# One assignment's one-hot products in two parts: the bank of the squares' sums and spare columns of a score tile

## The chip, the cores and the metric

The kernel runs on one core of one Trainium2 chip. The metric is the device time of one execution in microseconds (us); several executions are timed and their median is given. A core has five engines with an instruction stream each: PE (matrix products), DVE, ACT and POOL (elementwise work), and SP, which here only issues transfers. They wait for one another through semaphores.

## What is computed

Four batches of eight heads of attention, 768 positions with 64 values each, in which a query sees only keys of its own cluster; then a feed-forward network with the Mish function on the 3072 x 512 result.

```python
q_assign = np.argmax(np.einsum('bhsd,hcd->bhsc', q_n, c_n), axis=-1)
k_assign = np.argmax(np.einsum('bhsd,hcd->bhsc', k_n, c_n), axis=-1)
mask = q_assign[:, :, :, None] == k_assign[:, :, None, :]
scores = np.where(mask, scale * np.matmul(q, k.transpose(0, 1, 3, 2)), -1000000000.0)
attn = np.exp(scores - np.max(scores, axis=-1, keepdims=True))
attn = attn / (np.sum(attn, axis=-1, keepdims=True) + 1e-09)
x = np.matmul(attn, v)              # then to (3072, 512)
h = x @ w_in                        # (512, 2048)
sp = np.where(h > 20.0, h, np.log1p(np.exp(np.minimum(h, 20.0))))
g = h * np.tanh(sp)
out = g @ w_out                     # (2048, 512)
```

## The kernel before

**Units and score tiles.** The attention is cut into 96 units (a head and a third of its queries) of two halves of 128 queries. For unit i, half a, PE makes the scores in a PSUM tile s{i}_{a} of two banks: `scores_own` (L670) the products of q and k, `scores` (L690) on top of them the products of Z and T, whose last 16 rows are one-hot cluster rows, which stand for the mask. Of the 512 columns of each bank, scores fill 384; the other 128 are spare. DVE takes the row maximum m (`rowmax`, L701), ACT the exponential p (`expo`, L715). In the early units (0 to 23) PE transposes p into tiles q of the tag "H" (`p_lo`, L763), ACT and DVE copy these to SBUF (`ptrans`, L784 and L782), and `pv` (L806) multiplies with v for two units at a time into a tile o of the tag "M"; pv 10 covers units 20 and 21. Later units are transposed by DMA (L786). A half such as unit 22, half 0 is called s22_0, m22_0, exp22_0 and q22_0 below, by tile.

**Assignments.** For four heads at a time, PE multiplies q and k with the centroids (`assign_mm`, L572), DVE turns the result, takes the maximum over clusters and compares (`assign_turn`, `assign_max`, `assign_hot`, `assign_back`, L583 to L604), PE forms the one-hot rows of the four heads out of it (`assign_put`, L628), DVE evicts them into a tile stg (`assign_stg`, L649), and SP copies 16 rows at a time into Z and T of each head (`hot_copy`, L660 and L661). Assignment 2 serves heads 8 to 11, whose first scores are those of unit 24.

**PSUM.** Eight banks: tag "S" two tiles of two banks each (the scores, and put of the assignments after the first), "M" one bank, "H" two banks (the transposes q, later the products h of the first matrix, L901 to L903), "O" one bank. Early in the program "O" holds gram, the sums of squares of the weights (L323); from unit 28 on it holds the output O of the second matrix (L1038 to L1040). A ring hands out the tiles of a tag in the order of the program: who asks for one waits until its last reader is done.

**Other work beside it.** The weights are scaled and split into two 16-bit parts by POOL (`w_low` L295, `w_hi` L360), ACT (`w_abs` L286) and DVE (`w_f32` L303, `w_lo` L366); q and k of later heads are prepared by POOL (`prep`, L500 to L521); the values' squares go through `v_sq` (ACT, L384), `v_max` (DVE, L415), `v_cross` (PE, L389), `v_peak` (DVE, L393), `v_wide` (PE, L398) into one number that scales v. v_cross writes into spare columns of s22_1, v_wide into those of s23_0.

**What sets the order.** A list ORDER of 3408 steps, written out in the kernel, gives each step its rank. `Plan` issues steps by rank and ties the instructions of each engine in that order; `pl.after` issues a step's predecessors first. So a step that waits holds up everything behind it on its engine.

Of the kernel before, what the change touches and what calls it, by code (L numbers as in the profile page):

```python
# [1672 lines left out]
p_lo 15 0, scores 16 1, w_sq 25, w_sq 26, w_sq 27, w_sq 28, p_lo 15 1, scores 17 1, scores 17 0, recip 15 1, rowmax 16  # L1673
0, rowmax 16 1, ptrans 15 0, expo 16 0, p_hi 16 0, total 16 0, recip 16 0, expo 16 1, p_hi 16 1, w_lo 6, ptrans 15 1,
rowmax 17 0, rowmax 17 1, recip 14 1, p_lo 16 0, pv 7 0, pv 7 1, pv 7 2, pv_out 14, x_lo 14, p_lo 16 1, v_sq 1 0,
w_abs 30, w_abs 29, expo 17 0, p_hi 17 0, total 17 0, recip 17 0, ptrans 16 0, w_abs 31, expo 17 1, p_hi 17 1, ptrans
16 1, total 16 1, w_low 29, prep_hi 7, prep_lo 7, w_low 31, recip 16 1, w_f32 30, w_f32 29, w_f32 31, pv_out 15, x_lo
15, w_hi 7, total 17 1, scores 18 1, p_lo 17 0, scores 18 0, w_sq 29, p_lo 17 1, w_sq 30, rowmax 18 1, ptrans 17 0,
rowmax 18 0, ptrans 17 1, w_lo 7, pv 8 0, w_sq 31, recip 17 1, w_sum 1, expo 18 0, p_hi 18 0, total 18 0, recip 18 0,
p_lo 18 0, scores 19 0, w_spread 1, w_scale 1, rowmax 19 0, expo 18 1, p_hi 18 1, ptrans 18 0, p_lo 18 1, scores 19 1,  # L1680
pv 8 1, pv 8 2, pv_out 16, x_lo 16, rowmax 19 1, ptrans 18 1, expo 19 0, p_hi 19 0, total 19 0, recip 19 0, expo 19 1,
p_hi 19 1, copy_t 7, copy_z 7, qk_load 11, qk_load 10, hot_copy 7, copy_a 7, x_move 6 1, copy_b 7, x_move 5 0,
assign_mm 2, p_lo 19 0, scores 20 0, w_hi 8, total 19 1, total 18 1, w_lo 8, pv_out 17, x_lo 17, w_hi 9, recip 19 1,
recip 18 1, assign_turn 2, prep_hi 8, ptrans 19 0, prep_lo 8, p_lo 19 1, scores 20 1, assign_max 2, rowmax 20 0,
assign_hot 2, ptrans 19 1, rowmax 20 1, assign_back 2, expo 20 0, p_hi 20 0, total 20 0, recip 20 0, expo 20 1, p_hi
20 1, pv 9 0, p_lo 20 0, scores 21 0, pv 9 1, rowmax 21 0, w_lo 9, moe_scale_h 0, pv 9 2, pv_out 18, x_lo 18, scores
# [290 lines left out]
```

## Time and profile before

| what | value |
|---|---|
| median of three timed runs | 838.34 us (838.01 to 838.62) |
| the profiled execution's own time | 836.27 us |
| its span (first to last instruction) | 834.5 us |
| PE, DVE, ACT, POOL busy | 99%, 79%, 61%, 53% |
| granted TensorE clock | 1.00 over the whole span |

The profile is of one execution. Its span is 1.77 us shorter than its own time, and that time lies 2.07 us below the median of the timed runs. A row of the order-of-time view has the start, the duration, engine, line, operation, tiles (result, arrow, inputs), shape and count, and in brackets the idle time just before it with the instruction that ended it. Instructions of one kind in a row are put together, and durations overlap where an engine pipelines, so starts are the better measure of what an instruction takes.

### The profile page before, as it was taken

How to read it: one execution, taken by the hardware profiler on the slowest of the kernel's cores; microseconds unless marked ns; L12 is line 12 of the kernel's file. 1: busy time of each engine (PE TensorE's matmuls, PEld its weight loads, DVE VectorE, ACT ScalarE, POOL GpSimd, SP SyncE). 2: the span in 40 equal slices, each digit the busy share in tenths (PEclk: the TensorE clock that was granted, in tenths of full speed). 3: DMA queues.
4: the chain of work that ended last, by engine and by line, in shares of the span. 5: the costliest groups of instructions: out<-in, count | busy, mean ns of one | idle time of the engine just before them, and what ended most of it. 6: DMA issues, size and time to landing. Idle time of an engine off the chain costs nothing.

```text
span 834.5 us, 17572 instructions
## 1 busy us (share of the span) xinstructions
PE 822.7 (99%) x6732; PEld 624.9 (75%) x6733; DVE 659.9 (79%) x1146; ACT 509.6 (61%) x872; POOL 440.6 (53%) x424
## 2 busy tenths in 40 slices
PE   7999999999999999999999999999999999999998
PEld 3787777876776777776776687686777677788887
DVE  7999999999788868688777778778887675688822
ACT  6988877766565755573765465575665564365610
POOL 4778865976675555565656356665557251110000
PEclk9999999999999999999999999999999999999999
DMA  9997843899999968878899979896979774000001
GB/s 345 284 286 228 209 124 77 162 188 169 185 183 215 175 120 177 193 152 129 149 175 187 218 147 160 156 205 133 171 132 155 131 115 90 13 1 2 1 8 70
DMA packets 257299, 125.64 MB, mean 151 GB/s; under 512 B 231136, under 2 KB 234720, under 8 KB 257216
## 3 DMA queue, kind: packets, MB, share of 16 engines
q1 hardware_dynamic: 253120, 115.54, 66.5%
q10 hardware_dynamic: 4096, 8.98, 5.2%
q8 instruction: 53, 0.87, 0.4%
q14 instruction: 30, 0.25, 0.1%
HBM read 35.72 MB, written 6.29 MB: 50 GB/s over the span
## 4 chain that ended last, share of the span: by engine, by line
PE 85%; DVE 5%; ACT 3%; DMA 3%; POOL 2%; issue 2%; ACTq 0%; DVEq 0%; POOLq 0%; SPq 0%
PE o L806 10%; PE h L901 10%; PE h L903 10%; PE h L902 10%; PE O L1038 7%; PE O L1039 7%; PE O L1040 7%; PE s L670 7%; PE s L690 6%; PE cn L991 2%; PE q L763 1%; DVE m L701 1%; PE as L572 1%; ACT p L715 1%; DMA stage<-in_w_out_dram 1%
## 5 line engine op out<-in xcount | busy, mean ns | idle before, releaser
L715 ACT ACTIVATE p<-s,m 128x768 f32<-128x768 f32 x192 | 172.8, 902 | 112.1 <-DVE m L701 46.9
L753 POOL TENSOR_SCALAR hl<-p,l 128x768 f16<-128x768 f32 x144 | 164.6, 1147 | 142.9 <-DVE l L735 73.5
L701 DVE TENSOR_REDUCE m<-s 128x1 f32<-128x768 f32 x192 | 179.7, 949 | 47.5 <-PE s L690 46.2
L770 DVE SCALAR_TENSOR_TENSOR hl<-p,l,hl 128x768 f16<-128x768 f32 x144 | 173.9, 1218 | 25.0 <-POOL hl L753 24.0
L901 PE MATMUL h<-x,w 128*128 128x256 f16 x640 | 175.0, 273 | 0.2 <-ACT pt L784 0.2
L903 PE MATMUL h<-x,w 128*128 128x256 f16 x640 | 174.4, 273 | 0.0
L902 PE MATMUL h<-x,w 128*128 128x256 f16 x640 | 174.4, 273 | 0.0
L670 PE MATMUL s<-A,B 128*128 128x384 f32 x384 | 116.4, 384 | 2.4 <-ACT p L715 1.6
L1038 PE MATMUL O<-w,g 128*128 128x512 f16 x288 | 109.9, 382 | 0.0
L1039 PE MATMUL O<-w,g 128*128 128x512 f16 x288 | 109.2, 379 | 0.0
L1040 PE MATMUL O<-w,g 128*128 128x512 f16 x288 | 109.2, 379 | 0.0
L690 PE MATMUL s<-Z,T 80*128 80x384 f32 x384 | 99.3, 340 | 0.0
L901 PEld LDWEIGHTS <-w 128*128 128x128 f16 x768 | 75.1, 98 | 20.7 <-issue 9.9
L912 ACT ACTIVATE u<-h,msch 128x512 f32<-128x512 f32 x80 | 53.7, 686 | 50.8 <-PE h L903 38.0
L902 PEld LDWEIGHTS <-w 128*128 128x128 f16 x768 | 75.3, 98 | 10.9 <-issue 0.4
L903 PEld LDWEIGHTS <-w 128*128 128x128 f16 x768 | 75.2, 98 | 8.7
L918 POOL TENSOR_SCALAR g<-u,mscg 128x512 f16<-128x512 f32 x72 | 60.5, 844 | 36.7 <-ACT u L912 29.5
L806 PE MATMUL o<-pt,v 128*64 128x256 f16 x1296 | 77.6, 274 | 0.0
L806 PEld LDWEIGHTS <-v 128*64 128x64 f16 x1296 | 67.9, 110 | 9.8 <-issue 9.3
L926 DVE SCALAR_TENSOR_TENSOR g<-u,mscg,g 128x512 f16<-128x512 f32 x72 | 67.6, 946 | 9.7 <-POOL g L918 9.7
L670 PEld LDWEIGHTS s<-A,B 128*128 128x128 f32 x384 | 64.6, 190 | 13.6 <-ACT p L715 3.5
L690 PEld LDWEIGHTS s<-Z,T 80*128 80x128 f32 x384 | 70.0, 189 | 0.1
(251 smaller groups left out, 1347.1 us busy)
## 6 DMA issues: line engine op xcount, KB each, us to landing
qk<-in_qk_dram SPq DMA_DIRECT2D x32, 384.0 KB, 4.4
stage<-in_w_in_dram SPq DMA_DIRECT2D x16, 512.0 KB, 7.3
stage<-in_w_out_dram SPq DMA_DIRECT2D x16, 512.0 KB, 5.1
vraw<-in_vP_dram SPq DMA_DIRECT2D x16, 384.0 KB, 5.4
Z<-B SPq DMA_DIRECT2D x30, 192.0 KB, 3.5
out_dram<-osb SPq DMA_DIRECT2D x18, 256.0 KB, 3.3
T<-A ACTq DMA_DIRECT2D x23, 192.0 KB, 3.9
B<-T ACTq DMA_DIRECT2D x21, 192.0 KB, 4.0
```

Source lines behind the costliest of these rows:

```text
L670: nc.tensor.matmul(s[:, j, :384], st["B", n][:, q0 : q0 + P], st["A", n][:, j * 384 : (j + 1) * 384], start=True, stop=False, skip_group_c ...
L690: nc.tensor.matmul(st["s", i, a][:, j, :384], st["T", n][: D + NCL, q0 : q0 + P], st["Z", n][: D + NCL, j * 384 : (j + 1) * 384], start=Fa ...
L701: nc.vector.tensor_reduce(m, st["s", i, a][:, :, :384], axis=AX.XY, op=ALU.max, negate=True)
L715: nc.scalar.activation(p.rearrange("p (n x) -> p n x", n=2), st["s", i, a][:, :, :384], AF.Exp, bias=st["m", i, a], scale=1.0, accum_out=l,)
L770: nc.vector.scalar_tensor_tensor(t[:, 1], p, r, t[:, 0], op0=ALU.mult, op1=ALU.subtract)
L806: nc.tensor.matmul(o[s * D : s * D + D, :256], v if early else v[:, int(part == 1)], st["pt", 2 * m + s][:, :, c + (0 if early or part < 2 ...
L901: nc.tensor.matmul(o, wh, xh, start=(c == 0), stop=False)
L902: nc.tensor.matmul(o, wh, xl, start=False, stop=False)
L903: nc.tensor.matmul(o, wl, xh, start=False, stop=(c == 3))
L1038: nc.tensor.matmul(o, gh, wh, start=(f == 0 and fi == 0), stop=False)
L1039: nc.tensor.matmul(o, gh, wl, start=False, stop=False)
L1040: nc.tensor.matmul(o, gl, wh, start=False, stop=(f == 7 and fi == 1))
```

## The change

For the third assignment (q = 2) `assign_put` asks for no tile of the tag "S". Its first 512 columns go into a tile of the tag "O", the last 256 into the spare columns of both banks of s22_0, which has to be made first. That is three products (512, 128 and 128 columns) in place of two (512 and 256), and `assign_stg` evicts it in two instructions in place of one. The other assignments stay as they were. The lines behind it move by 6 to 8 numbers (L628 is L634, L649 is L657, L670 is L678, L701 is L709, L715 is L723, L763 is L771, L784 is L792).

```diff
@@ -605,7 +605,13 @@
 
     def assign_put(q):
         pl.after(("assign_back", q), ("put_consts",))
-        if q:
+        if q == 2:
+            pl.after(("scores", 22, 0))
+            o = ps.tile([P, 512], F32, tag="O", name=f"put{q}", bufs=T["O"])
+            t = st["s", 22, 0][:, :, 384:]
+            st["put", q] = [(o, 0, 512), (t, 512, S)]
+            parts = [(o, 0, 512), (t[:, 0], 512, 640), (t[:, 1], 640, S)]
+        elif q:
             o = ps2.tile([P, 1024], F32, tag="S", name=f"put{q}")
             st["put", q] = [(o[:, :S], 0, S)]
             parts = [(o[:, :512], 0, 512), (o[:, 512:S], 512, S)]
@@ -646,7 +652,9 @@
         pl.after(("assign_put", q))
         stg = op1.tile([P, S], F32R, tag="stg", name=f"stg{q}")
         for o, c0, c1 in st["put", q]:
-            nc.vector.tensor_scalar(stg[:, c0:c1], o, 0.0, put_b, op0=ALU.max, op1=ALU.subtract)
+            t = stg[:, c0:c1]
+            t = t.rearrange("p (j x) -> p j x", j=2) if len(o.shape) == 3 else t
+            nc.vector.tensor_scalar(t, o, 0.0, put_b, op0=ALU.max, op1=ALU.subtract)
         st["stg", q] = stg
 
     def hot_copy(n):
...
```

Of the list ORDER, 340 places change (581 to 920 of 3408, from the 15th unit's end to the second pair of the feed-forward's first product); the steps are the same. The two lines with the put and the eviction, before and now:

```diff
-rowmax 21 1, w_lo 10, rowmax 22 0, ptrans 20 1, expo 21 1, p_hi 21 1, p_lo 21 0, assign_put 2, p_lo 21 1, ptrans 21 0,
-v_sq 1 3, expo 22 0, p_hi 22 0, total 22 0, recip 22 0, assign_stg 2, v_max 1, ptrans 21 1, scores 22 1, v_cross 1,
...
+21 1, rowmax 22 0, w_lo 10, ptrans 20 1, expo 21 1, p_hi 21 1, assign_put 2, p_lo 21 0, p_lo 21 1, scores 22 1, ptrans
+21 0, assign_stg 2, moe_scale_h 0, expo 22 0, ptrans 21 1, p_hi 22 0, total 22 0, recip 22 0, pv 10 0, v_cross 1, p_lo
...
```

**First place: POOL, about 100 to 109 us.** Names: stage holds raw weights (w_low, L295), qk, A and B belong to head 7 (prep). Before:

```order
L295 TENSOR_SCALAR stage_1400<-stage_1400 128x512
L500 TENSOR_SCALAR qk_478<-qk_478,scq 128x768
L503 TENSOR_SCALAR A_1650<-qk_478 128x768
L521 TENSOR_TENSOR B_1653<-qk_478,A_1650 128x768
L295 TENSOR_SCALAR stage_1405<-stage_1405 128x512
```

Now:

```order
L500 TENSOR_SCALAR qk_478<-qk_478,scq 128x768
L503 TENSOR_SCALAR A_1647<-qk_478 128x768
L521 TENSOR_TENSOR B_1650<-qk_478,A_1647 128x768
L295 TENSOR_SCALAR stage_1400<-stage_1400 128x512
L295 TENSOR_SCALAR stage_1405<-stage_1405 128x512
```

The three instructions of prep stand ahead of both weight pieces; before they stood between them, so the second piece (stage_1405) was behind all of them and the first piece too.

**Second place: PE around the put.** Names: s_1_1922 and s_0_1935 before, s_1_1920 and s_0_1925 now are s21_1 and s22_0; s_1_1996 and s_1_1983 are s22_1; q_0_0, q_0_3, q_1_0 and q_1_3 are the transposes of one half in two tiles, first of unit 20, half 1, then of unit 21. Weight loads are left out. Before:

```order
L670 MATMUL s_1_1922<-A_1650,B_1653 128x384 x2
L690 MATMUL s_1_1922<-Z_1796,T_1794 128x384 x2
L763 MATMUL q_1_0_1927<-ident,p_1_1883 128x128 x3
L763 MATMUL q_1_3_1931<-ident,p_1_1883 128x128 x3
L670 MATMUL s_0_1935<-A_1650,B_1653 128x384 x2
L690 MATMUL s_0_1935<-Z_1796,T_1794 128x384 x2
L763 MATMUL q_0_0_1963<-ident,p_0_1943 128x128 x3
L763 MATMUL q_0_3_1967<-ident,p_0_1943 128x128 x3
L628 MATMUL put_1971<-hott_1878,put_w 128x512
L628 MATMUL put_1971<-hott_1878,put_w 128x256
L763 MATMUL q_1_0_1974<-ident,p_1_1961 128x128 x3
L763 MATMUL q_1_3_1978<-ident,p_1_1961 128x128 x3
```

Now:

```order
L678 MATMUL s_0_1925<-A_1647,B_1650 128x384 x2
L698 MATMUL s_0_1925<-Z_1800,T_1798 128x384 x2
L771 MATMUL q_1_0_1930<-ident,p_1_1885 128x128 x3
L771 MATMUL q_1_3_1934<-ident,p_1_1885 128x128 x3
L634 MATMUL put_1963<-hott_1880,put_w 128x512
L634 MATMUL s_0_1925<-hott_1880,put_w 128x128
L634 MATMUL s_0_1925<-hott_1880,put_w 128x128
L771 MATMUL q_0_0_1967<-ident,p_0_1941 128x128 x3
L771 MATMUL q_0_3_1971<-ident,p_0_1941 128x128 x3
L771 MATMUL q_1_0_1975<-ident,p_1_1961 128x128 x3
L771 MATMUL q_1_3_1979<-ident,p_1_1961 128x128 x3
L678 MATMUL s_1_1983<-A_1647,B_1650 128x384 x2
```

s22_0 has moved ahead of the transposes of unit 20, the put stands ahead of those of unit 21 instead of between them, and two of its products write the tile of s22_0.

**Third place: DVE around the eviction, and ACT beside it.** Names: m_1_1954 is m21_1, m_0_1957 and m_0_1956 are m22_0, m_1_2033 and m_1_2039 are m22_1; w_951 is the split of a weight piece (w10), vsm belongs to v_max, pt to the copies of the transposes. DVE before:

```order
L701 TENSOR_REDUCE m_1_1954<-s_1_1922 128x1
L366 SCALAR_TENSOR_TENSOR w_951<-w_780,ws1r,w_951 128x1024
L701 TENSOR_REDUCE m_0_1957<-s_0_1935 128x1
L649 TENSOR_SCALAR stg_1990<-put_1971,put_b 128x768
L415 TENSOR_REDUCE vsm_1992<-vm_1284 128x1
L782 COPY pt_1982<-q_1_3_1978 128x384
L366 SCALAR_TENSOR_TENSOR w_780<-w_1085,ws1r,w_780 128x1024
L701 TENSOR_REDUCE m_1_2033<-s_1_1996 128x1
```

DVE now:

```order
L709 TENSOR_REDUCE m_1_1954<-s_1_1920 128x1
L709 TENSOR_REDUCE m_0_1956<-s_0_1925 128x1
L366 SCALAR_TENSOR_TENSOR w_951<-w_780,ws1r,w_951 128x1024
L657 TENSOR_SCALAR stg_1991<-put_1963,put_b 128x512
L657 TENSOR_SCALAR stg_1991<-s_0_1925,put_b 128x256
L463 TENSOR_SCALAR msch_1994<-vs0r,ws0r 128x1
L467 TENSOR_SCALAR mscg_1996<-vs0r,ws0r 128x1
L790 COPY pt_1988<-q_1_3_1979 128x384
L366 SCALAR_TENSOR_TENSOR w_780<-w_1085,ws1r,w_780 128x1024
L709 TENSOR_REDUCE m_1_2039<-s_1_1983 128x1
```

m22_0 has moved ahead of w10, the eviction is in two and stays behind w10, v_max has left, and the two small products msch and mscg came in. ACT before, from exp21_1 to exp22_1:

```order
L715 ACTIVATE p_1_1961,l_1944<-s_1_1922,m_1_1954 128x768
L784 COPY pt_1982<-q_0_0_1963 128x384
L784 COPY pt_1982<-q_0_3_1967 128x384
L384 ACTIVATE vq_3_1985,vm_1284<-vraw_3_1408 128x768
L715 ACTIVATE p_0_1987,l_1988<-s_0_1935,m_0_1957 128x768
L784 COPY pt_1982<-q_1_0_1974 128x384
L784 COPY pt_2059<-q_0_0_2002 128x384
L784 COPY pt_2059<-q_0_3_2006 128x384
L715 ACTIVATE p_1_2062,l_1988<-s_1_1996,m_1_2033 128x768
```

ACT now:

```order
L723 ACTIVATE p_1_1961,l_1942<-s_1_1920,m_1_1954 128x768
L792 COPY pt_1988<-q_0_0_1967 128x384
L792 COPY pt_1988<-q_0_3_1971 128x384
L723 ACTIVATE p_0_1998,l_1999<-s_0_1925,m_0_1956 128x768
L792 COPY pt_1988<-q_1_0_1975 128x384
L723 ACTIVATE p_1_2061,l_1999<-s_1_1983,m_1_2039 128x768
```

By the semaphores of the changed program, the two short products of the put wait for m22_0, exp22_0 waits for the second eviction (before: for m22_0 alone), and s22_1 waits for no eviction (before: for stg). The square vq_3 has left this stretch, and exp22_1 stands ahead of the copies of unit 22's transposes. On PE the first four products of pv 10 now stand between s22_1 and v_cross; before, all of pv 10 stood behind s23_0. On SP, two loads of qk (L490) that stood around the first transpose by DMA of unit 24 (L786) now both stand ahead of it. In the rest of the 340 places the halves of units 25 to 27, tiles of h and steps of e_mish, e_gh and e_gl change places with their neighbours.

## Rows read from the trace of the kernel before

**Rows 1.** Page, parts 1 and 4: busy time, and the chain that ended last

```profile
PE 822.7 (99%) x6732; PEld 624.9 (75%) x6733; DVE 659.9 (79%) x1146; ACT 509.6 (61%) x872; POOL 440.6 (53%) x424
...
PE 85%; DVE 5%; ACT 3%; DMA 3%; POOL 2%; issue 2%; ACTq 0%; DVEq 0%; POOLq 0%; SPq 0%
```

**Rows 2.** Busy time by stretch: PE, PEld, DVE, ACT, POOL, PEclk, DMA, GB/s

```profile
90.00:118.00 28.00, 27.39 (x236) 21.71 (x237) 26.28 (x42) 24.09 (x57) 18.14 (x20) 1.00 0.72 188
118.00:148.00 30.00, 28.50 (x221) 21.51 (x215) 28.02 (x52) 19.88 (x47) 19.96 (x22) 1.00 0.26 60
148.00:170.00 22.00, 22.00 (x208) 19.30 (x205) 20.36 (x32) 17.27 (x28) 19.20 (x16) 1.00 0.96 176
```

**Rows 3.** Waits of PE in 95 to 175 us: total, times, longest

```profile
PE s L670 <- DVE vsm L415: 0.7, 1, 0.7
PE q L763 <- ACT pt L784: 0.5, 2, 0.3
...
PE put L628 <- ACT p L715: 0.2, 1, 0.2
```

**Rows 4.** PE in order of time, 129 to 144 us: start, duration, then [idle before]

```profile
129.34 0.82 PE L763 MATMUL q<-ident,p 128*128 128x128 f32 x6
130.40 0.48 PE L628 MATMUL put<-hott,put_w 128*128 128x512 bf16 x2 [0.25 <-ACT p L715]
130.77 0.93 PE L763 MATMUL q<-ident,p 128*128 128x128 f32 x6
132.39 0.62 PE L670 MATMUL s<-A,B 128*128 128x384 f32 x2 [0.69 <-DVE vsm L415]
133.31 0.82 PE L763 MATMUL q<-ident,p 128*128 128x128 f32 x6
133.88 0.59 PE L670 MATMUL s<-A,B 128*128 128x384 f32 x2
134.75 1.95 PE L806 MATMUL o<-pt,vraw 128*64 128x256 f32 x16
136.63 0.38 PE L398 MATMUL s<-vsm,ones 1*128 1x1 f32 x2
...
143.60 0.27 PE L901 MATMUL h<-x,w 128*128 128x256 f16 x1 [0.19 <-ACT pt L784]
```

**Rows 5.** PE, 109 us: the transposes of score tile 17, half 1

```profile
109.99 0.93 PE L763 MATMUL q<-ident,p 128*128 128x128 f32 x6 [0.27 <-ACT pt L784]
```

**Rows 6.** POOL and DVE, 107 to 109 us

```profile
107.08 0.98 POOL L295 TENSOR_SCALAR stage<-stage 128x512 uint32<-128x512 uint16 x1
...
108.09 0.69 DVE L303 SCALAR_TENSOR_TENSOR w<-w,stage 128x512 uint32<-128x512 uint32 x1 [0.54 <-POOL stage L295]
```

**Rows 7.** DVE, 128 to 135 us

```profile
129.05 1.50 DVE L366 SCALAR_TENSOR_TENSOR w<-w,ws1r,w 128x1024 f16<-128x1024 f32 x1
130.47 0.94 DVE L701 TENSOR_REDUCE m<-s 128x1 f32<-128x768 f32 x1
131.33 1.00 DVE L649 TENSOR_SCALAR stg<-put,put_b 128x768 fp32r<-128x768 f32 x1
...
134.84 0.27 DVE L393 TENSOR_REDUCE vsm<-s 1x1 f32<-1x128 f32 x1
```

**Rows 8.** ACT, 131 to 136 us

```profile
131.80 0.93 ACT L715 ACTIVATE p<-s,m 128x768 f32<-128x768 f32 x1
...
132.68 0.51 ACT L784 COPY pt<-q 128x384 f32<-128x384 f32 x1
...
135.21 0.90 ACT L715 ACTIVATE p<-s,m 128x768 f32<-128x768 f32 x1 [0.51 <-DVE vsm L393]
```

**Rows 9.** DVE at 18 us: the same eviction of assignment 0, two instructions

```profile
18.33 1.13 DVE L649 TENSOR_SCALAR stg<-put,put_b 128x512 fp32r<-128x512 f32 x2
```

**Rows 10.** SP's issues, 128 to 149 us

```profile
134.22 0.59 SPq L490 DMA_DIRECT2D qk<-in_qk_dram  x1
...
149.14 1.39 SPq L786 DMA_TRANSPOSE pt<-hl  x1
```

More of the change, by code (lines that the diff above doesn't have):

```diff
@@ L1672 @@
 w_low 27, w_hi 5, w_low 28, w_f32 27, w_lo 5, w_f32 28, total 15 1, w_hi 6, pv_out 13, x_lo 13, total 14 1, w_low 30,
[L1673 to L1686, printed above, removed]
@@ L1797 @@
[L1797 to L1801 removed]
+p_lo 15 0, scores 16 1, w_sq 25, w_sq 26, w_sq 27, w_sq 28, p_lo 15 1, scores 17 1, scores 17 0, rowmax 16 0, rowmax
@@ new lines @@
+21 0, assign_stg 2, moe_scale_h 0, expo 22 0, ptrans 21 1, p_hi 22 0, total 22 0, recip 22 0, pv 10 0, v_cross 1, p_lo
+22 0, scores 23 0, pv 10 1, w_hi 11, total 21 1, copy_z 8, copy_t 8, copy_a 8, x_move 8 1, hot_copy 8, x_move 8 0,
+copy_b 8, w_lo 11, rowmax 22 1, recip 21 1, v_peak 1, total 20 1, rowmax 23 0, recip 20 1, v_wide 1, scores 23 1, pv
+10 2, pv_out 20, x_lo 20, expo 22 1, ptrans 22 0, expo 23 0, p_hi 22 1, p_hi 23 0, total 23 0, recip 23 0, w_hi 12,
+prep_hi 9, p_lo 22 1, w_lo 12, rowmax 23 1, expo 23 1, ptrans 22 1, p_hi 23 1, v_scale 1, w_hi 13, w_lo 13, total 23
@@ new lines @@
+1, w_hi 14, pv_out 21, total 22 1, prep_lo 9, x_lo 21, scores 24 1, scores 24 0, p_lo 23 0, p_lo 23 1, m1 0 0, rowmax
+24 1, rowmax 24 0, ptrans 23 0, w_lo 14, recip 22 1, ptrans 23 1, recip 23 1, expo 24 1, expo 24 0, scores 25 1,
+scores 25 0, pv 11 0, pv 11 1, pv 11 2, m1 0 1, m1 1 0, m1 1 1, pv_out 22, x_lo 22, scores 26 1, scores 26 0, m1 3 0,
+m1 3 1, m1 2 0, m1 2 1, total 24 0, recip 24 0, rowmax 25 1, rowmax 25 0, total 24 1, p_hi 24 0, w_hi 15, copy_t 9,
+expo 25 1, expo 25 0, recip 24 1, p_lo 24 0, w_lo 15, v_high 1 0, p_hi 24 1, pv_out 23, total 25 1, total 25 0, p_lo
@@ new lines @@
+ptrans 44 0, copy_z 16, ptrans 45 1, ptrans 45 0, x_move 18 1, hot_copy 16, pv_out 43, v_sq 2 3, copy_a 16, m_out 1 1,
+expo 46 1, e_mish 20, copy_b 16, e_mish 21, x_lo 43, e_gl 19, total 46 1, recip 46 1, rowmax 47 0, e_gl 18, rowmax 46
+0, rowmax 47 1, p_hi 46 1, e_gh 20, e_gh 21, prep_hi 17, pv 22 0, pv 22 1, pv 22 2, pv_out 44, x_lo 44, m1 23 1,
+scores 48 0, scores 48 1, m1 22 0, m1 22 1, expo 47 0, expo 46 0, pv_out 45, expo 47 1, v_sq 2 2, e_mish 22, e_mish
+23, copy_t 17, total 47 0, e_gl 20, recip 47 0, p_lo 46 1, x_lo 45, total 47 1, recip 47 1, total 46 0, recip 46 0,
@@ new lines @@
+m2 3 0 0, m2 3 0 1, m1 33 0, e_mish 31, pv_out 51, expo 54 1, expo 54 0, e_mish 29, p_lo 53 0, x_lo 51, e_gl 30, total
+54 1, recip 54 1, v_split 2 1, total 54 0, recip 54 0, p_lo 53 1, rowmax 55 1, rowmax 55 0, p_hi 54 0, e_gh 29, p_hi
+54 1, x_move 23 1, ptrans 52 1, copy_z 19, m_store 2 1, ptrans 52 0, qk_load 22, hot_copy 19, ptrans 53 0, ptrans 53
+1, assign_mm 5, m1 32 0, scores 56 1, scores 56 0, pv 26 0, pv 26 1, pv 26 2, pv_out 52, x_lo 52, expo 55 1, expo 55
+0, p_lo 54 0, e_gl 29, p_lo 54 1, total 55 1, total 55 0, recip 55 0, recip 55 1, assign_turn 5, assign_max 5,
@@ new lines @@
+1, pv 27 2, pv_out 54, x_lo 54, m2 3 0 7, scores 59 0, scores 59 1, m2 3 1 0, m2 3 1 1, m1 34 0, m1 35 0, m1 35 1,
+scores 58 1, m1 34 1, expo 58 0, copy_t 20, expo 57 1, expo 57 0, pv_out 55, m_out 3 0, copy_b 20, e_mish 32, copy_a
+20, e_mish 33, total 58 0, recip 58 0, total 57 1, total 57 0, recip 57 0, recip 57 1, p_hi 58 0, p_hi 57 1, p_hi 57
+0, e_gh 33, prep_hi 21, e_gh 32, prep_lo 21, p_lo 58 0, x_lo 55, p_lo 57 0, rowmax 59 0, p_lo 57 1, rowmax 59 1,
+v_split 2 2, rowmax 58 1, ptrans 56 1, x_move 26 0, ptrans 56 0, m_store 3 0, hot_copy 20, ptrans 57 0, ptrans 57 1,
```

215 lines of the change are left out of this document (102 added, 113 removed).

## The prediction

> **What bounds the kernel now.** I read the page's first part and its chain first: PE is busy for 99% of the span and carries 85% of the chain that ended last [rows 1]. Whatever is taken off another engine is worth only what PE stands idle for because of it. So the second view is busy time by stretch. From 90 to 118 us PE lacks 28.00 - 27.39 = 0.61 us, from 118 to 148 us 30.00 - 28.50 = 1.50 us, and from 148 to 170 us nothing [rows 2]. The change reorders steps between about 97 and 170 us, so it works on 2.11 us of profiled idle time. The granted clock is 1.00 in each of these stretches, the 2.4 GHz level, so no term for the clock enters.
>
> The waits of PE name what that idle time is [rows 3]. The largest is one wait of 0.7 us of scores. The view puts it down to the small reduction vsm, but that is the instruction behind the eviction on DVE, which ends when the wait does. In order of time [rows 4] the reader sees the put at 130.40, with 0.25 us of idle time before it, and the scores s22_1 at 132.39, with 0.69 us. Starts say more than modelled ends. A group of six transposes that nothing holds up takes 133.88 - 133.31 = 0.57 us from its start to the next start. The group at 129.34 should have been followed at 129.91 and was at 130.40: 0.49 late. The one at 130.77 should have been followed at 131.34 and was at 132.39: 1.05 late. So the ring of score tiles costs 1.54 us here. The put waits for exp21_1 to leave its tile, then s22_1 waits for the eviction to leave the put's. Starts show 1.54 / 0.94 = 1.6 times the marked idle time of these two places, and with that factor all gaps of both stretches come to about 2.11 x 1.6 = 3.4 us. No reordering can gain more than that here.
>
> **The parts, and what each costs.** The sum is made against the profiled execution of 836.27 us, and then set on the median of 838.34, 2.07 above it.
>
> *One more product and its weight load.* 256 columns are now two times 128: the same columns. The put's two products took 130.77 - 130.40 = 0.37 us [rows 4]. A third costs between 0 and half of that; I take 0.1.
>
> *One more eviction instruction.* The trace has the same pair: assignment 0 was evicted as 512 and 256 columns in 1.13 us [rows 9], against 1.00 for 768 in one [rows 7]. So DVE pays 0.13 more. Beside PE it is free as long as nobody on the path waits for the end of it.
>
> *POOL's order near 100 us.* DVE idles 0.54 us for a weight piece that POOL starts at 107.08, behind the preparation of head 7 [rows 6]. What DVE does next goes by ACT's cast and copies to PE, whose transposes of unit 17 idle 0.27 us at 109.99 [rows 5]. With that preparation earlier, the wait goes. The gain is between 0.27 (PE's marked idle time) and 0.54 (DVE's); I take 0.4.
>
> *The put's own two waits.* Both go as they stand: the put needs no score tile, and s22_1 follows exp21_1 alone. By the old order the work up to 129.34 would now end at 128.94, and the 512-column product starts there. The two short ones wait for m22_0. DVE did w10 at 129.05 and m22_0 at 130.47 [rows 7]; now m22_0 comes first, at 129.05 - 0.4 = 128.65, and takes 131.33 - 130.47 = 0.86 to 129.51. The short products follow at about 129.6. The second transposes of unit 21 still wait for ACT's copies of the first, so they start between 130.77 and 131.1, and s22_1 between 131.34 and 131.65. I take the later one, since ACT's copies for unit 20 now also come later. So s22_1 is 132.39 - 131.65 = 0.74 us early.
>
> *What is late next.* Here the gain is lent, not kept. exp22_0 now waits for the second eviction, because that reads the tile it reads. DVE ends m22_0 at 129.51, w10 takes 130.47 - 129.05 = 1.42 to 130.93, the two evictions 1.13 to 132.06. exp22_0 started at 131.80 before [rows 8], with ACT full ahead of it; now about 132.0, though its maximum is there at 129.51. Behind it on ACT is the copy for unit 21, 132.68 - 131.80 = 0.88 after it, at 132.9, and 0.51 long: 133.4. The first products of pv 10, now right behind s22_1, need that copy. PE is through with s22_1 at 131.65 plus 0.80 (132.39 to v_cross at 133.19) = 132.45 and stands until 133.4: a new stall of 0.95. Then come four products of pv 10 (4/16 of 136.63 - 134.75 = 0.47), v_cross, transposes, s23_0 (0.87, from 133.88 to 134.75) and m23_0 (0.94), which v_wide needs: about 136.45, against 136.63 before. On DVE, m22_1 and v_peak end the same chain near 134.7, against 134.84, and exp22_1 waits for v_peak as before [rows 7, 8]. From v_wide on, ACT's exponentials and copies lead to the first h at 143.60 as they did. So about 0.2 us is left at h.
>
> *SP and the steps behind 143 us.* A load of qk now stands ahead of the first transpose by DMA of unit 24; before, one was issued at 134.22, long before that transpose at 149.14 [rows 10], and one behind it. PE is full from 148 to 170 us, and DMA 0.96 [rows 2]. The cover is PE's other work in that full stretch, so it costs nothing; if the cover is gone, PE waits for the transpose behind a load, and the rival of missed slots below has that price.
>
> Sum: -0.4 from POOL's order, -1.54 from the put's waits, +0.1 for the product, and the rest, about +1.6, given back at pv 10 and v_wide, which leaves -0.2. That is 836.1 for the profiled execution and **838.1 us** on the median. Unknowns between -0.8 and +0.7 put this case at 837.3 to 839.0.
>
> A rule speaks against the change. The Trainium skill, "PSUM — Partial Sum Buffer", Terms, says that two engines must not be on the same bank at once, reads against reads included. By it, put, maximum, eviction and exponential on s22_0 go strictly one after another, whatever columns they touch. That is how the sum above has it; no row of the kernel before shows a put beside scores.
>
> **Rivals.** *The gain is kept.* If exp22_0 does not start later than 131.80, or the stall at pv 10 only fills time that PE would have stood anyway, the two waits (1.54) and the POOL wait (0.27 to 0.54) come through at v_wide, less 0.1: -1.7 to -2.0, **836.5 us**. For it: the waits are PE's largest here [rows 3]. Against: v_wide needs m23_0, and exp22_1 needs v_peak, which DVE reached late already.
>
> *The exponential becomes the bound.* Place: exp22_0 behind the two evictions behind w10. If m22_0 cannot start before its old 130.47, for instance because s22_0 is itself held by its ring slot, then w10 ends at 130.47 + 0.86 + 1.42 = 132.75 and the evictions at 133.9, exp22_0 is 2.1 late, the copy is at 134.8 to 135.3, and v_cross at 135.3 + 0.47 = 135.8 and v_peak near 135.9 against 134.84. That is +1.1, **839.4 us**. It decides once m22_0 starts later than about 129.5. For it: DVE is busy for 28.02 of 30 us there [rows 2], so it cannot catch up. Against: m22_0 has moved ahead of w10.
>
> *A slot is missed in the full stretch.* The halves and h tiles of units 25 to 28 change places where PE has no idle time at all [rows 2], so the reorder can only lose. Two misses of one exponential each (0.93 [rows 8]) give +1.9, **840.2 us**. Against: each ring is asked for in the same number and kind.
>
> **How the numbers follow.** 0.2% of 838.34 is 1.7 us, about what a measurement of this kernel can tell from no change: faster is below 836.7, slower above 840.0. Forecast 0.58, all of it within 0.2% but 0.02 on the fast side. Gain kept 0.22, nearly all of it faster, as it lies just below the bound: 0.20 faster, 0.02 same. Exponential 0.12: 0.09 same, 0.03 slower. Missed slots 0.08, all slower. That is faster 0.22, same 0.67, slower 0.11. The range takes in the kept gain from 836.4 on, and the exponential's case to 839.7; outside are the missed slots and the rest of these tails, 2 in 10.
>
> **What would show it.** Right: no idle time at s22_1, but 0.5 us or more before the first product of pv 10 released by ACT's copy; exp22_0 within 0.4 us of 131.8 and released by the eviction; v_wide near 136.4; the first h 0 to 0.5 us early; 148 to 170 us full. Gain kept: pv 10 without a stall and h at 142 or before. Exponential: exp22_0 after 133, v_peak after 135.5. Missed slots: PE idle behind 148 us. What would make the whole forecast wrong is a difference that arises outside 97 to 170 us, as a later ring slot that catches the shifted work.

## The result and the profile after

The changed kernel takes 841.27 us (median of six runs, 840.27 to 844.05); the kernel before, timed beside it, 837.56 (six runs). The ratio is 1.0051, 95% interval 1.0039 to 1.0064: slower, by 3.7 us between the medians, where no measurable change was forecast, and outside the range. The profiled execution of the changed kernel took 844.05 us, the longest of the six, with a span of 842.3.

Page, part 1, changed kernel:

```profile
PE 825.7 (98%) x6733; PEld 626.1 (74%) x6734; DVE 660.5 (78%) x1147; ACT 510.2 (61%) x872; POOL 443.7 (53%) x424
```

Against [rows 1] no engine has notably more to do. Of PE's 3.0 us more busy time, about half comes with one stretch at a lower clock (last section). What has grown besides is waiting.

Busy time by stretch, changed kernel, columns as in [rows 2], the last stretch new:

```profile
90.00:118.00 28.00, 26.92 (x227) 21.56 (x229) 25.29 (x44) 24.64 (x57) 20.03 (x21) 1.00 0.71 194
118.00:148.00 30.00, 28.47 (x218) 21.03 (x215) 27.07 (x47) 19.55 (x45) 19.53 (x20) 1.00 0.19 42
148.00:170.00 22.00, 20.72 (x177) 17.81 (x176) 18.55 (x31) 15.41 (x23) 18.75 (x16) 1.00 0.92 159
172.60:176.00 3.40, 3.40 (x34) 2.92 (x35) 1.68 (x2) 1.59 (x3) 2.05 (x2) 0.50 1.14 263
```

PE lacks 1.08 us from 90 to 118 (before 0.61), 1.53 from 118 to 148 (1.50), and 1.28 from 148 to 170, where nothing was missing [rows 2]. What it waits for, as in [rows 3]:

```profile
PE o L814 <- DMA pt<-hl: 2.2, 1, 2.2
PE q L771 <- ACT pt L792: 1.4, 3, 0.7
PE h L909 <- ACT u L920: 1.3, 1, 1.3
PE s L634 <- DVE m L709: 0.3, 1, 0.3
```

The put's waits of 0.7 and 0.2 us are gone, as meant. In their place stand the transposes' waits for ACT's copies, the put's short products' wait for a maximum, and behind 148 us an h that waits for u and a product that waits for a transpose by DMA.

The start of an execution varies: the squares' sums at 109 us began between 109.0 and 110.6 in the profiles of this study, in one (mended) at 112.7. So I measure from there: to the first h (the **middle**), and from it to the centroids' products of assignment 3 (the **tail**), by starts on PE in one profile each:

| kernel | first h | middle | tail | span |
|---|---|---|---|---|
| before | 143.60 | 34.28 | 47.96 | 834.5 |
| changed, first profile | 145.17 | 35.63 | 53.49 | 842.3 |
| changed, second profile (changed_look) | 146.07 | 35.60 | 49.79 | 840.4 |

The middle loses 1.3 us, the tail 1.8 in the second profile; the first also has a long wait at 172 us. Profiles of programs that are the same up to h agree in the middle to 0.05 us, once only to 0.4 (tail_old below). Tails are less sharp: the ten kernels below and above that have the old order behind 143 us show 47.94 to 49.13. That second span is 5.9 over the one before: 1.15 from the start, 1.32 middle, 1.83 tail, 1.60 later.

**The middle.** Changed kernel in order of time; 0.22 us come off to compare with rows of before (109.54 against 109.32 for the squares' sums). PE:

```profile
110.68 0.93 PE L771 MATMUL q<-ident,p 128*128 128x128 f32 x6 [0.73 <-ACT pt L792]
...
130.09 0.38 PE L634 MATMUL put<-hott,put_w 128*128 128x512 bf16 x1
130.80 0.27 PE L634 MATMUL s<-hott,put_w 128*128 128x128 bf16 x2 [0.33 <-DVE m L709]
...
132.13 0.93 PE L771 MATMUL q<-ident,p 128*128 128x128 f32 x6 [0.40 <-ACT pt L792]
...
133.69 0.65 PE L814 MATMUL o<-pt,vraw 128*64 128x256 f32 x2
134.50 1.08 PE L814 MATMUL o<-pt,vraw 128*64 128x256 f32 x6 [0.16 <-ACT pt L792]
135.50 0.27 PE L389 MATMUL s<-ident,vsm 128*1 128x128 f32 x1
...
138.18 0.38 PE L398 MATMUL s<-vsm,ones 1*128 1x1 f32 x2
```

DVE and ACT:

```profile
128.93 1.81 DVE L709 TENSOR_REDUCE m<-s 128x1 f32<-128x768 f32 x2
130.66 1.27 DVE L366 SCALAR_TENSOR_TENSOR w<-w,ws1r,w 128x1024 f16<-128x1024 f32 x1
131.85 0.74 DVE L657 TENSOR_SCALAR stg<-put,put_b 128x512 fp32r<-128x512 f32 x1
132.51 0.47 DVE L657 TENSOR_SCALAR stg<-s,put_b 128x256 fp32r<-128x256 f32 x1
...
135.81 0.96 DVE L709 TENSOR_REDUCE m<-s 128x1 f32<-128x768 f32 x1 [0.92 <-PE s L389]
```

```profile
133.08 0.90 ACT L723 ACTIVATE p<-s,m 128x768 f32<-128x768 f32 x1 [0.62 <-DVE stg L657]
133.98 0.47 ACT L792 COPY pt<-q 128x384 f32<-128x384 f32 x1
```

The reader sees the chain that was forecast, later than forecast. exp22_0 waits for the second eviction, which stands behind w10. Behind it is the copy that pv 10 needs, so PE's start at 134.50 is 0.81 behind one at 133.69 that had two short products. v_wide is at 137.96 on before's clock, against 136.63.

**The first part**, 101 to 110 us, POOL and then DVE:

```profile
101.28 1.76 POOL L500 TENSOR_SCALAR qk<-qk,scq 128x768 f32<-128x768 f32 x1
...
105.95 2.27 POOL L295 TENSOR_SCALAR stage<-stage 128x512 uint32<-128x512 uint16 x2
108.30 0.97 POOL L735 TENSOR_SCALAR l<-l 128x2 f32<-128x2 f32 x2
```

```profile
107.02 0.69 DVE L303 SCALAR_TENSOR_TENSOR w<-w,stage 128x512 uint32<-128x512 uint32 x1 [0.60 <-POOL stage L295]
108.26 0.69 DVE L303 SCALAR_TENSOR_TENSOR w<-w,stage 128x512 uint32<-128x512 uint32 x1 [0.55 <-POOL stage L295]
109.30 0.17 DVE L741 RECIPROCAL l<-l 128x2 f32<-128x2 f32 x1 [0.36 <-POOL l L735]
```

Where DVE waited 0.54 us for one weight piece [rows 6], it waits 0.60 and 0.55 for two, then 0.36 for a small product that POOL has behind both: 1.51 in all. The transposes of unit 17 start 1.14 behind the squares' sums (110.68 - 109.54) instead of 0.67 [rows 5].

**The tail.** POOL, SP and PE of the changed kernel:

```profile
157.09 0.91 POOL L761 TENSOR_SCALAR hl<-p,l 128x768 f16<-128x768 f32 x1 [2.32 <-DMA pt<-hl]
...
161.23 2.06 POOL L926 TENSOR_SCALAR g<-u,mscg 128x512 f16<-128x512 f32 x2
```

```profile
150.18 1.07 SPq L490 DMA_DIRECT2D qk<-in_qk_dram  x2
151.36 1.39 SPq L794 DMA_TRANSPOSE pt<-hl  x1
```

```profile
164.66 0.27 PE L909 MATMUL h<-x,w 128*128 128x256 f16 x1 [1.28 <-ACT u L920]
```

The two loads stand ahead of the transpose. POOL's next hl needs a tile that the transpose still reads, and waits 2.32 us; g follows behind it on POOL, then DVE's part of g, ACT's next u, and h, which waits for its tile.

### The profile page after: what moved, and what is told of

Read it like the earlier page. It is cut to its first block, busy times and chain, and to the rows that moved or that the text cites. A ratio compares the mean times of both kernels' runs of the same rounds, so it can differ in the third digit from the quotient of the medians.

```text
span 842.3 us, 17576 instructions
## 1 busy us (share of the span) xinstructions
PE 825.7 (98%) x6733; PEld 626.1 (74%) x6734; DVE 660.5 (78%) x1147; ACT 510.2 (61%) x872; POOL 443.7 (53%) x424
## 4 chain that ended last, share of the span: by engine, by line
PE 78%; DMA 2%; POOL 0%; issue 0%; DVE 0%; ACTq 0%; ACT 0%; POOLq 0%; DVEq 0%
PE h L909 9%; PE h L910 9%; PE h L911 9%; PE o L814 9%; PE O L1046 8%; PE O L1048 7%; PE O L1047 7%; PE s L678 6%; PE s L698 6%; PE cn L999 2%; DMA pt<-hl 2%; PE cy('k', 1)_10945 L1193 1%; PE cy('k', 0)_10699 L1193 1%; PE as L572 1%; PE cx('k', 1)_10946 L1193 1%; PE ca('k', 0)_10698 L1193 1%
## 5 line engine op out<-in xcount | busy, mean ns | idle before, releaser
L723 ACT ACTIVATE p<-s,m 128x768 f32<-128x768 f32 x192 | 172.8, 902 | 113.3 <-DVE m L709 45.9
L761 POOL TENSOR_SCALAR hl<-p,l 128x768 f16<-128x768 f32 x144 | 162.9, 1135 | 149.0 <-DVE l L743 74.9
L709 DVE TENSOR_REDUCE m<-s 128x1 f32<-128x768 f32 x192 | 179.7, 949 | 49.2 <-PE s L698 46.6
L678 PE MATMUL s<-A,B 128*128 128x384 f32 x384 | 116.3, 384 | 2.2 <-ACT p L723 2.1
L814 PE MATMUL o<-pt,v 128*64 128x256 f16 x1296 | 79.5, 277 | 2.2 <-DMA pt<-hl 2.2
L678 PEld LDWEIGHTS s<-A,B 128*128 128x128 f32 x384 | 64.6, 190 | 13.7 <-ACT p L723 4.7
```

Of the source, the lines that this page charges most:

```text
L678: nc.tensor.matmul(s[:, j, :384], st["B", n][:, q0 : q0 + P], st["A", n][:, j * 384 : (j + 1) * 384], start=True, stop=False, skip_group_c ...
L709: nc.vector.tensor_reduce(m, st["s", i, a][:, :, :384], axis=AX.XY, op=ALU.max, negate=True)
L723: nc.scalar.activation(p.rearrange("p (n x) -> p n x", n=2), st["s", i, a][:, :, :384], AF.Exp, bias=st["m", i, a], scale=1.0, accum_out=l,)
L814: nc.tensor.matmul(o[s * D : s * D + D, :256], v if early else v[:, int(part == 1)], st["pt", 2 * m + s][:, :, c + (0 if early or part < 2 ...
```

## The experiments

My theory after the result: the middle loses by its new chain, the first part by POOL, the tail by the loads; the losses are separate and add up. The rivals: one early lateness does it all, or the placement itself costs nothing and only the order does. Every ratio is to the kernel before, timed beside it; its medians were 836.94, 837.05, 836.79 and 837.12 us in the four groups below. The ratios are not the quotients of the medians (put_only's would be 1.0022). "Middle" and "tail" are as in the table above.

**One stretch put back, or alone.** Each edit is to the list ORDER (its places counted from 0; counted so, 277 places between 581 and 918 hold another step, not 340 as the section on the change has it); a last edit moves the loads only.

```diff
-ORDER of the changed kernel
+first_old: its places before 663 as before
+tail_old: its places from 812 as before
+mid_only: both of these, so only places 663 to 811 and the code are new
+loads_back: ptrans 24 0 between qk_load 15 (put ahead of copy_z 9) and qk_load 12, as before
```

> The changed kernel with the old order up to the second squares (the stretch before about 113 us); everything behind it stays changed. Theory A (losses add: POOL's new order costs about 0.7 us at 110 us, the put region 0.8, the part behind 143 us the rest of the 3.7): 840.6, that is 0.7 less than the changed kernel's 841.3; q of unit 17, half 1 waits 0.3 us again, not 0.7. Theory B (the stretch behind 148 us is a cliff: what matters is only how late its tiles arrive): 838.5 or below. Theory C (POOL's order costs nothing, the shift at 110 us is spread between executions): 841.3.

> The changed kernel with the old order from the first product of the feed-forward (about 143 us) on; the put in two parts and all the order ahead of it stay changed. Theory A (the new order behind 143 us makes the two new stalls, 1.3 us at the products h5 and 2.2 us at pv 12, itself): about 839.0 to 839.5, PE full from 148 to 172 us. Theory B (these stalls come from arriving 1.5 us late, not from the order): 841 or more, with the stalls still there.

> The kernel before, with only the put in two parts and the new order between about 113 and 143 us; old order ahead of and behind it. Theory A (the put region loses 0.8 us by its new chain: eviction, exponential, copy, pv 10): 838.4, 0.8 more than the kernel before of the same call. Theory B (the put region gains, its late start in the changed kernel came from POOL): 836.8, 0.8 less than before. The first product of h would stand at 144.4 by A and at 143.0 by B, against 143.6.

> The changed kernel with nothing but the two loads of qk back at their old places among SP's issues (one ahead of the copies of head 9, one behind the first transpose of unit 24). Theory A (the loads ahead of that transpose delay it, and with it the ring of hl and pv 12): 839.0, pv 12 waits less than 0.5 us for a transpose. Theory B (the transposes are late because the halves they take are late): 841.3, the wait at pv 12 stays at about 2 us.

| kernel | us | ratio, 95% interval | middle | tail |
|---|---|---|---|---|
| first_old | 839.87 | 1.0034, 1.0023 to 1.0045 | 35.11 | 51.02 |
| tail_old | 839.48 | 1.0030, 1.0020 to 1.0040 | 35.98 | 48.28 |
| mid_only | 838.44 | 1.0020, 1.0010 to 1.0030 | 35.16 | 49.04 |
| loads_back | 839.78 | 1.0032, 1.0019 to 1.0045 | 35.62 | 48.90 |

No single piece brings the time back: first_old, tail_old and loads_back each take some 0.2% off the 0.51%. mid_only keeps 0.20%: 0.9 us are lost at the first h, and its tail is another 1.1 us longer, in the old order; why, no run shows. first_old's tail of 51.02 holds a wait for a transpose at pv 12 of 1.38 us. In loads_back, whose only difference is where two loads stand, the wait of h for u is gone (the two waits of PE in 155 to 240 us):

```profile
PE s L678 <- ACT p L723: 0.6, 1, 0.6
PE o L814 <- DMA pt<-hl: 0.5, 1, 0.5
```

**One stretch alone in the kernel before, and two mends of the middle.**

```diff
-ORDER of the kernel before
+first_only: its places before 663 as changed
+tail_only: its places from 812 as changed
-ORDER of mid_only: rowmax 22 0, w_lo 10, ptrans 20 1, ... assign_stg 2, moe_scale_h 0
+evict_first: rowmax 22 0, ptrans 20 1, ... assign_stg 2, w_lo 10, moe_scale_h 0
-ORDER of mid_only: pv 10 0, v_cross 1
+cross_first: v_cross 1, pv 10 0
```

> The kernel before with nothing but the new order of the first part (POOL's preparation of head 7 ahead of both weight pieces, ACT's square later), up to about 113 us; the put as before. Theory A (losses add, this part costs 0.5 to 0.9 us): 837.6 to 837.9 where the kernel before has 837.0; the transposes of unit 17, half 1 wait 0.7 us instead of 0.3. Theory B (this part costs only together with the new middle): 837.0.

> The kernel before with nothing but the new order from the first product of h (143 us) on; the put and everything ahead of it as before. Theory A (the order itself makes the stalls at h5 and pv 12): 838.5 to 839, with a wait of about 1 us at h5 for ACT and one at pv 12 for a transpose. Theory B (it needs the 1.5 us of lateness as well): 837.0 to 837.3 and no such waits.

> The kernel with the new middle alone (mid_only), with the two evictions of the put ahead of the weight split w10 on DVE in place of behind it. Theory A (everything behind the put hangs on exp22_0, which waits for the second eviction, which waits behind w10): exp22_0 starts 0.6 to 0.8 us earlier, and from the squares' sums at 109 us to the first product of h it takes 34.4 instead of 35.2 us (the kernel before: 34.3); time 0.8 below mid_only. Theory B (the maximum m22_1, which now waits for v_cross behind pv 10, is what counts; exp22_0 is covered): no more than 0.3 below.

> The kernel with the new middle alone, with v_cross ahead of the first four products of pv 10 in place of behind them. Theory A (exp22_0 is what counts): m22_1 starts about 1 us earlier, but s23_0 and v_wide stay within 0.1 us, and the first product of h comes 0 to 0.3 us earlier. Theory B (m22_1 behind v_cross is what counts): the first product of h comes 0.8 us earlier, 34.4 us behind the squares' sums at 109 us.

| kernel | us | ratio, 95% interval | middle | tail |
|---|---|---|---|---|
| first_only | 836.82 | 1.0000, 0.9991 to 1.0010 | 34.76 | 47.94 |
| tail_only | 839.95 | 1.0026, 1.0017 to 1.0034 | 34.29 | 49.45 |
| evict_first | 837.65 | 1.0004, 0.9995 to 1.0013 | 34.63 | 48.45 |
| cross_first | 838.37 | 1.0016, 1.0007 to 1.0025 | 35.10 | 48.93 |

The first part alone is 0.48 us late at h, and as late at the end of the tail (47.94 against 47.96). Its time shows no loss, but an interval of 0.1% on either side is 0.8 us and can't exclude 0.48. The tail alone costs 0.26%. So mid_only and tail_only together make 0.46%, near the whole; one early lateness, the rival, is out. evict_first shows the mechanism of the middle. ACT and PE in it (0.31 us come off to compare with before):

```profile
131.88 0.95 ACT L723 ACTIVATE p<-s,m 128x768 f32<-128x768 f32 x1
```

```profile
133.25 1.16 PE L814 MATMUL o<-pt,vraw 128*64 128x256 f32 x8
...
137.27 0.38 PE L398 MATMUL s<-vsm,ones 1*128 1x1 f32 x2 [0.28 <-DVE m L709]
```

With the evictions ahead of w10, exp22_0 no longer waits for DVE (no idle time in its row) and pv 10 runs its eight products without a stall. That gives back 0.53 of the 0.88 us at h, and most of the time (0.04% is left of 0.20%). What is left is DVE's work in another place: w11 waits 0.55 us for POOL's part of it (at 133.80), and v_wide 0.28 for m23_0. cross_first lets v_cross, for which m22_1 waited 0.92 us, go first: m22_1 comes 1.03 us earlier, and h gains 0.06. That wait was covered.

**Placement against order; loads against order.**

```diff
-the changed kernel's ORDER
+put_only: ORDER of the kernel before, with the changed put and eviction
-ORDER of the kernel before: qk_load 15, x_move 9 1, copy_z 9, ptrans 24 0, qk_load 12
+loads_only: x_move 9 1, copy_z 9, qk_load 15, qk_load 12, ptrans 24 0
-ORDER of tail_only: copy_z 9, hot_copy 9, qk_load 15, qk_load 12, ptrans 24 0
+tail_loads: qk_load 15, copy_z 9, hot_copy 9, ptrans 24 0, qk_load 12
-ORDER of mid_only
+mended: the moves of evict_first and cross_first, and w_lo 11 behind v_peak 1
```

> The kernel before in its own order, with nothing but the put in two parts and its eviction in two. Theory A (the placement itself puts exp22_0 behind the evictions): DVE still does w10, m22_0, evictions in this order, so the short products wait for m22_0 until about 131.4, exp22_0 starts near 132.7 in place of 131.8, the transposes of unit 22 near 134.1 in place of 133.3, and the first product of h 34.9 to 35.1 us behind the squares' sums at 109 us in place of 34.3; time 0.6 to 0.8 above the kernel before. Theory B (the placement frees a score tile and costs nothing; only the new order costs): equal to the kernel before or up to 0.5 below.

> The kernel before with nothing but the two loads of qk moved ahead of the first transpose by DMA of unit 24. Theory A (these loads ahead of the transpose make the loss behind 143 us): 838.5, 1.5 above the kernel before, with a wait of PE for ACT at h4 or one for a transpose at pv 12. Theory B (the loads cost only with the changed order of h5, h4 and the halves): 837.0 to 837.4.

> The kernel before with the new order from 143 us on, but the two loads of qk at their old places. Theory A (the loads make the loss there): 837.0 to 837.5, no wait of 1 us at h5. Theory B (the order of halves, h tiles and pv 12 makes it): 838.5 to 840, the wait at h5 stays.

> The new middle alone (old order ahead of 113 and behind 143 us), mended at three places: the evictions ahead of w10, v_cross ahead of pv 10, and the weight split w11 behind v_peak on DVE, so that m22_1 starts about 1.7 us earlier. If exp22_0 behind the eviction was the loss and the put in two parts is worth anything, this is its best form: 34.2 to 34.4 us from the squares' sums to the first product of h, 836.8 to 837.2, no slower than the kernel before. If the short products' wait for m22_0 and the second half's wait for ACT's copies (0.33 and 0.41 us in evict_first) cost what the old waits cost, it will not get below the kernel before.

| kernel | us | ratio, 95% interval | middle | tail |
|---|---|---|---|---|
| put_only | 838.67 | 1.0014, 0.9998 to 1.0030 | 35.34 | 48.29 |
| loads_only | 837.12 | 0.9997, 0.9982 to 1.0012 | 34.31 | 48.49 |
| tail_loads | 837.87 | 1.0011, 0.9994 to 1.0029 | 34.31 | 48.52 |
| mended | 838.28 | 1.0018, 1.0001 to 1.0036 | 34.99 | 48.88 |

put_only is 1.06 us late at h though nothing is reordered. Of this, 0.30 was there ahead of anything that the edit touches: the transposes of unit 17 began 0.97 behind the squares' sums (before 0.67), after a product of POOL (L521) of 2.81 us where the kernel before has 2.19. The other 0.76 is the placement's, so by the rows the rival that only the order costs is out; by time alone it isn't, as the interval begins below 1. The rows also say where, PE, ACT and DVE (0.30 come off to compare with before):

```profile
132.06 0.27 PE L634 MATMUL s<-hott,put_w 128*128 128x128 bf16 x2 [1.09 <-DVE m L709]
...
132.42 0.91 ACT L723 ACTIVATE p<-s,m 128x768 f32<-128x768 f32 x1
...
133.45 0.48 DVE L657 TENSOR_SCALAR stg<-s,put_b 128x256 fp32r<-128x256 f32 x1 [0.78 <-ACT p L723]
```

The short products wait for the maximum of the tile that they borrow, but PE loses nothing by that: s22_1 starts at 132.45 on before's clock, with the 0.30 in it, against 132.39. Theory A's path is not what happened either. exp22_0 starts at 132.12 on that clock, only the 0.30 late, and waits for nobody: in the old order it stands ahead of the eviction, so here the second eviction waits for the exponential, 0.78 us. Behind it on DVE, m22_1 and v_peak come 1.29 late, the 0.30 in it (135.27 and 136.13 against 133.98 and 134.84), and v_wide 1.07. The two readers of the one tile follow each other in either order, and whichever is second is late.

The loads alone and the new tail alone are both within what can be measured by time; with both, it is 0.26%. The three intervals overlap, and the tails are 0.53 (loads), 0.56 (order) and 1.49 us (both) longer than before's, so each half may cost some. What only both together show is h waiting long for u, and POOL's hl shows why. loads_only, then tail_only, then tail_loads, each POOL in order of time:

```profile
154.80 0.90 POOL L753 TENSOR_SCALAR hl<-p,l 128x768 f16<-128x768 f32 x1 [1.46 <-DMA pt<-hl]
...
158.06 0.69 POOL L918 TENSOR_SCALAR g<-u,mscg 128x512 f16<-128x512 f32 x1
```

```profile
155.47 0.91 POOL L753 TENSOR_SCALAR hl<-p,l 128x768 f16<-128x768 f32 x1 [1.74 <-DMA pt<-hl]
...
159.61 2.05 POOL L918 TENSOR_SCALAR g<-u,mscg 128x512 f16<-128x512 f32 x2
```

```profile
153.92 1.60 POOL L753 TENSOR_SCALAR hl<-p,l 128x768 f16<-128x768 f32 x1
```

The loads make POOL wait for the transpose (1.46 and 1.74; without them none). The new order puts an hl ahead of both g that stood between them, so the first g is at 159.61 with both, and at 158.06 where only the loads moved. h then waited 0.97 us for u in tail_only, 0.36 in loads_only, and not at all in tail_loads. The one profile of loads_only is 1.2 us longer than that of before (836.0 - 834.5, less 0.34 of the start): 0.53 in the tail, and 0.66 at a wait of scores for ACT at 224 us, 1.30 where the kernel before has 0.64. That its timed runs show no loss stays open. mended is no better than evict_first by time; its profiled execution took 844.28 us, 6 above its median, and I read no more from it.

**The two waits without the new wait.** The short part of the put goes into a tile of the tag "M" of its own, so nothing of it touches s22_0.

```diff
 put_m: the changed code, ORDER of the kernel before, and
-            t = st["s", 22, 0][:, :, 384:]
-            st["put", q] = [(o, 0, 512), (t, 512, S)]
-            parts = [(o, 0, 512), (t[:, 0], 512, 640), (t[:, 1], 640, S)]
+            t = ps2.tile([P, 512], F32, tag="M", name=f"put{q}m", bufs=1)[:, :256]
+            st["put", q] = parts = [(o, 0, 512), (t, 512, S)]
 put_m_order: the same, with w_lo 10 behind assign_stg 2, w_lo 11 behind v_peak 1,
 v_sq 1 0 and v_sq 1 3 behind ptrans 18 1, v_max 1 behind rowmax 20 0
```

> The kernel before in its own order, with the put's 512 columns in the bank of the squares' sums and the other 256 in the bank of pv (tag M), which is free between pv 9 and pv 10: no score tile is touched. Theory A (the loss of the put in two parts is exp22_0 behind the evictions; the removed waits are real but covered by DVE's m22_1 and v_peak): no wait in front of the put and s22_1 about 0.7 to 1 us earlier, but v_wide and the first product of h within 0.2 us of the kernel before, 34.1 to 34.4 us behind the squares' sums; time equal to the kernel before within 0.5. Theory B (any put outside of the score ring costs, through its third pass or the second eviction): 35 us and 838. Theory C (the waits were worth their 1.5 us): 33.2 us and 835.5.

> put_m, with the weight splits w10 and w11 moved behind the evictions and behind v_peak on DVE, and the squares of v earlier on ACT, so that exp22_0, m22_1 and v_peak can start 0.7 to 1 us earlier. Theory A: the first product of h 33.4 to 34.0 us behind the squares' sums (0.3 to 0.9 earlier than in the kernel before), time 836.2 to 836.6, if nothing later gives it back. Theory B: no earlier than the kernel before.

> The changed kernel, profiled once more. If the wait of 2.2 us at pv 12 and the clock of 0.94 behind it belong to the change, they are there again, and from the first product of h to the centroid products of assignment 3 it takes 53 us; if they belong to that one execution, the wait at h5 (1.3 us) stays, pv 12 waits 1 us or less, the clock is 1.00 and it takes 49.5 to 50.5 us (the kernel before: 47.96).

| kernel | us | ratio, 95% interval | middle | tail |
|---|---|---|---|---|
| put_m | 837.37 | 1.0005, 0.9996 to 1.0014 | 34.20 | 48.71 |
| put_m_order | 839.30 | 1.0026, 1.0017 to 1.0035 | 35.50 | 49.13 |

PE of put_m (0.37 us come off to compare with [rows 4]):

```profile
131.86 0.59 PE L676 MATMUL s<-A,B 128*128 128x384 f32 x2
...
133.54 0.85 PE L769 MATMUL q<-ident,p 128*128 128x128 f32 x6 [0.28 <-DVE pt L788]
...
136.93 0.38 PE L398 MATMUL s<-vsm,ones 1*128 1x1 f32 x2
```

Both waits of the put are gone and s22_1 starts at 131.49 on before's clock, 0.90 early. v_wide is at 136.56, against 136.63, and h gains 0.08. The gain ends at 133.54, where the next transposes wait for a copy that DVE has behind the same evictions; DVE's m22_1 is 0.15 later than before (134.13 against 133.98). So the two waits were never the bound: DVE's work, 28.02 of 30 us there [rows 2], joins PE's again two steps on. put_m_order moved DVE's weight pieces out of the way and only met them elsewhere (v_wide waited 0.51 for the maximum); it was also 0.6 us late ahead of the put already (transposes at 128.60 on before's clock, against 127.97). No version that I ran beats the kernel before.

changed_look is one more profile of the changed kernel (842.27 us). Its waits of PE in 155 to 240 us:

```profile
PE s L678 <- ACT p L723: 1.3, 1, 1.3
PE h L909 <- ACT u L920: 1.0, 1, 1.0
PE s L678 <- DVE stg L657: 0.5, 1, 0.5
PE o L814 <- DMA pt<-hl: 0.4, 1, 0.4
```

The 2.2 us wait for the transpose is 0.4 here and the clock was 1.00 throughout. With the same order, first_old waited 1.38 there and tail_only not at all, so the size of this wait changes from execution to execution. The wait of h for u is in all four. The first line is at 228 us, and it goes with the loads, not with the lateness of the tail: it is 1.1 to 1.6 us in all five profiles with both loads ahead of the transpose, loads_only among them, and 0.5 to 1.0 in the others but mended's. How the loads reach that far is not shown.

## Why the prediction was wrong

**The first term had the wrong sign.** "-0.4 from POOL's order" came as +0.47 (1.14 - 0.67 behind the squares' sums). The prediction priced the one wait that it saw and not what the moved steps put behind them: POOL's small product behind both weight pieces, and DVE behind that. The preparation itself also took longer where it now stands, 4.67 us (101.28 to 105.95) against 4.18 (102.90 to 107.08); one of its rows is in the last section. first_old undoes it (the wait at the transposes is back to 0.27, the middle 0.52 shorter).

**The middle's mechanism was right.** exp22_0 waited for the second eviction as worked out. Without the first term it was to start at 132.46; in mid_only it did at 132.36 (133.44 less 1.08 of the start). Of the terms that follow, one was mis-sized and a second perhaps:

- The products of pv 10 ahead of v_cross are eight in the trace (2 + 6), where I counted four from the order's rows, as the section on the change says too. From the end of the stall to v_cross took 1.00 us, not 0.47. Six of the eight stand behind the stall; at the 1.88 / 16 us of one product in [rows 4] they make 0.70, and the other 0.30 no row explains.
- The short products waited 0.33 for the maximum and the next transposes 0.40 for ACT's copies, so s22_1 was 0.29 us early in mid_only (133.18 - 1.08 = 132.10, against 132.39), not 0.74. If those 0.74 have the 0.4 of the first term in them, the forecast without it is 0.34, and this is no miss. Behind the stall it no longer matters.

In the changed kernel exp22_0 was at 132.86 on before's clock, 0.86 behind the forecast: all of it the first term (0.47 + 0.4). With 0.53 for the products that makes 1.39 of the 1.55 us by which the first h missed its forecast (144.95 against 143.40). From v_wide to h took 6.99 us, before 6.97, as forecast.

**"Given back at pv 10 and v_wide" was too kind to the waits.** -1.54 for the put's two waits was written as a gain lent. put_m shows that it was none: without them and without the new wait, 0.08 us. The bound of 3.4 us of gaps was no gain to be had either, since DVE is nearly as full as PE there. The rival "gain kept" falls with the same run.

**"SP loads 0" failed.** The named cover, PE's full stretch, was there and did not help, since the wait came over POOL: the ring of hl tiles, not the products that read the transpose. Its place is that of the rival of missed slots: priced +1.9, measured +1.83 at the end of the tail (changed_look) and 0.26% alone, with a chance of 0.08. That the sizes agree is luck: the price was two waits of an exponential each, and what came was POOL's wait for a transpose, in a tail that is good to about 1 us. The long wait of h for u needs the loads and the order together: loads_back and tail_loads lack the loads, loads_only lacks the order.

**The rivals were treated as exclusive.** The exponential's rival (+1.1; its condition, m22_0 after 129.5, was met with 129.58, by POOL's lateness and not by a ring slot; v_peak came at 136.54) and the missed slots (+1.9) lie in different stretches, and a loss came in both: 3.0 by their prices, where the range reached to the first of them alone. The measured difference is 3.7.

Of the rule that was weighed against the change (the Trainium skill, "PSUM — Partial Sum Buffer", Terms: two engines not on one bank at once) no run here decides: exp22_0 waits for the eviction of other columns of its tile by the program's semaphores, whatever the chip would allow.

## What to carry to other kernels

A wait in front of the busiest engine is worth taking away only if no other engine's chain meets it again a few steps on: follow the engine that is nearly as full to its next join before a gain is written down. A tile shared with a tensor on the critical chain puts the guest's readers into that chain; price the reader that comes second, behind everything ahead of it on its engine, in whichever order the two stand. Count instructions from rows of the trace, follow a load moved ahead in a queue to the ring whose tile it holds back, and add up the prices of rivals that lie in different stretches.
